# Sums of weight blocks made in place, raw w2 tiles, and bias and early preparation in the m1 steps of a two-layer-pair kernel

## The chip, the cores and the metric

One core of one Trainium2 chip runs the whole program. The metric is the device time of one execution in microseconds, as the median of several runs.

## The reference

Two kinds of layer alternate, each twice, with a residual sum around each. S = 2048 tokens, D = 1024, F = 3584, all float32.

```python
def A(q, k, v, shift_k, ssm_k, ssm_D):       # q is the layer norm of x
    kv = short_causal_conv(k, shift_k) * v   # 4 taps per channel
    y = long_causal_conv(kv, ssm_k)          # 2048 taps per channel, by FFT in the reference
    return q * (y + kv * ssm_D)

def B(x, w1, b1, w2, b2):                    # x is the layer norm of x
    h = einsum("bsd,df->bsf", x, w1) + b1
    h = where(h > 0, h, 0) ** 2
    return einsum("bsf,fd->bsd", h, w2) + b2

x = x + A(ln(x)); x = x + B(ln(x)); x = x + A(ln(x)); x = x + B(ln(x))
```

The result of the long convolution is the same in both A layers, so the kernel computes it once.

## The kernel before

**Blocks.** Tokens go in four blocks of 512, and each layer pair A, B handles a block at a time. `ORDER` lists the eight blocks (layer pair, token block): block 0 is (0, 0), and blocks 5, 6, 7 are (0, 3), (1, 2), (1, 3). The long convolution runs beside blocks 0 to 4; its products are made on GpSimd (POOL) and its other work on all engines. It is finished early in the second half of block 4.

**Steps.** A block is a list of steps, each with one weight tile of 128 x 512. An m1 step multiplies a w1 tile with the normalized input `xh`, `xl` (12 matmuls). Numbers are split into a high and a low fp32r part, and three matmuls make one product (`mm3`). After two m1 steps (kh = 0, 1) one F tile of 128 rows is complete, and `relu2` or `relu_w` makes its squared ReLU, `rh`, `rl`.

**Blocks 5 to 7 (`WINO`)** use a 2 x 2 block product with seven products in place of eight, as Strassen and Winograd did. Their F tiles go in pairs, `WCH = (3, 3, 4, 4)` pairs to a chunk. In each chunk the m1 steps come first (12, 12, 16, 16), and then seven groups j of w2 steps, one step per pair (21, 21, 28, 28 steps, 6 matmuls each), which accumulate in two PSUM banks. `evict_w` adds these to `acc` (or `fx`, `fg`) after each group. Three of the seven groups use w2 tiles as they are; four use sums of w2 blocks ("t" tiles, tensors `td`).

**Weights.** A weight goes one of two ways. Raw: SyncE (SP) loads 256 KB into `wr` (eight buffers) up to `W_LOAD` = 8 steps ahead, ScalarE (ACT) casts it to the high part of `whl` (six buffers), and VectorE (DVE) subtracts to make the low part; this pair of operations is the split. Pair: a split that was stored in DRAM (`wd_m1_...`, `wd_m2_...`, `wd_t_...`) is loaded whole, 512 KB, `W_PAIR` = 4 steps ahead. `from_pair` decides; about half of the weights are kept as pairs. A pair's load waits until PE has ended the step that used its buffer.

**What sets the order.** There is no scheduler in these blocks: the loop over steps writes all instructions, and each engine and SP's DMA queue runs its own in that order. `lag.at(k, f)` calls f k ticks later; a tick is a step, with a few more at the first w2 step of a chunk, which waits for `relu_w`. So SP, which issues every load and store, is one queue in order: a DMA that waits for an engine holds back all that stand behind it.

**Other work in these blocks.**
- `load_b2`, `add_b2w`: loads b2 (broadcast over partitions) into a `px` buffer, and POOL adds it to the residual in `acc` and `fk` (eight additions of 128 x 512).
- `prep_a`: from step 29 of a block on, loads the next block's four input token tiles into `px` (two buffers) and makes their statistics (`stats`), three steps apart.
- `prep_w`: the rest of the next block's preparation. `early` loads x and the convolution's result y (`YD`), combines them (`combine`, four operations), makes new statistics and stores x to `X1`. `late` loads `X1`, normalizes, transposes on PE and splits into the next `xh`, `xl`.
- `make_t`: makes the "t" tiles in 28 parts, each with two loads of w2 (256 KB), four differences of 128 x 256 on DVE and two stores (256 KB) to `TD`. It is a generator, advanced once per step from the convolution's end on.

In the weight buffers' names, wd_m1_1_2_1 is the pair of w1, F tile 7 x 1 + 2, half kh = 1.

Of the kernel before, what the change touches and what calls it, by code (L numbers as in the profile page):

```python
# [233 lines left out]
def tile_h3_mlp(ctx: ExitStack, tc: tile.TileContext, q, kT, vT, shk, ssmT, ssmD, w1, b1, w2, b2,  # L234
# [556 lines left out]

    def load_xy(l, b, tt):
        x, y = load_x(l, b, tt), []
        for h in range(2):
            yt = ml.tile([P, 512], F32, name="yt", bufs=2)
            SY.dma_start(yt, YD[b][:, tt, h * 512:(h + 1) * 512])
            y.append(yt)
        return x, y

    def combine(x, y, m, r):  # L800
        for h in range(2):
            sl = slice(h * 512, (h + 1) * 512)
            V.scalar_tensor_tensor(y[h], x[:, sl], m, y[h], op0=OP.subtract, op1=OP.mult)
            V.scalar_tensor_tensor(x[:, sl], y[h], r, x[:, sl], op0=OP.mult, op1=OP.add)
# [594 lines left out]
    def make_t():  # L1399
        parts = [(p, dq) for p in range(FT // 2) for dq in range(2)]  # L1400
        got = {}

        def load(n):
            if n < len(parts):
                p, dq = parts[n]
                got[n] = []
                for e in range(2):
                    pool, nm, m = (const, ("fh", "fl")[e], 1) if n % 2 else (cv, "sm", 2)
                    t = pool.tile([P, 2, 256], F32, name=nm, bufs=m)
# [7 lines left out]
        yield
        yield
        yield
        for n, (p, dq) in enumerate(parts):  # L1420
# [9 lines left out]
            yield  # L1430
            SY.dma_start(TD[p][:, 0:2, dq * 256:(dq + 1) * 256], t[0])
            yield
            SY.dma_start(TD[p][:, 2:4, dq * 256:(dq + 1) * 256], t[1])
            load(n + 2)
# [420 lines left out]
```

## Time and profile before

| | us |
|---|---|
| median of three runs | 2807.38 |
| the three runs | 2803.62, 2807.38, 2811.40 |
| the profiled execution | 2809.33 |
| its span, first to last instruction | 2807.6 |
| TensorE busy in the span | 2706.5 |
| granted TensorE clock, mean | 0.987 |

DMA moved 782.04 MB, 279 GB/s over the span. Block 4 begins at about 1560 us of the span, block 5 at 1877.8, block 6 at 2202.4, block 7 at 2508. In the views PE is TensorE, DVE VectorE, ACT ScalarE, POOL GpSimd; SPq is SP's DMA queue. A line of the windows view gives the stretch, its length, busy time (and count) of PE, PEld, DVE, ACT and POOL, then the granted clock, the share of time that the DMA engines were busy, and GB/s. A line of the waits view gives who waited for whom, the sum in us, how often, and the longest. A line of the timeline gives start, duration, engine, line, operation, and in brackets the idle time before it with what ended it.

### The profile page before, as it was taken

How to read it: one execution, taken by the hardware profiler on the slowest of the kernel's cores; microseconds unless marked ns; L12 is line 12 of the kernel's file. 1: busy time of each engine (PE TensorE's matmuls, PEld its weight loads, DVE VectorE, ACT ScalarE, POOL GpSimd, SP SyncE). 2: the span in 40 equal slices, each digit the busy share in tenths (PEclk: the TensorE clock that was granted, in tenths of full speed). 3: DMA queues.
4: the chain of work that ended last, by engine and by line, in shares of the span. 5: the costliest groups of instructions: out<-in, count | busy, mean ns of one | idle time of the engine just before them, and what ended most of it. 6: DMA issues, size and time to landing. Idle time of an engine off the chain costs nothing.

```text
span 2807.6 us, 36324 instructions
## 1 busy us (share of the span) xinstructions
PE 2706.5 (96%) x12532; PEld 2237.1 (80%) x12532; DVE 1942.1 (69%) x3009; ACT 1067.6 (38%) x1835; POOL 926.4 (33%) x655
## 2 busy tenths in 40 slices
PE   7799899799999999999999999999999999999999
PEld 6688787688888788888888888887777778777887
DVE  8868789777777877779767754366576655664545
ACT  4254344333334233442234322243335433343433
POOL 6826665155542555336552553001000000001000
PEclk9999999999999999999999999999999999999999
DMA  8589999789988898888977786778988876776565
GB/s 259 167 288 356 363 330 322 259 269 353 298 280 304 281 338 283 274 320 289 353 247 274 292 308 218 237 265 312 339 271 293 290 243 235 239 251 228 202 214 199
DMA packets 380025, 782.04 MB, mean 279 GB/s; under 512 B 43832, under 2 KB 160704, under 8 KB 379840
## 3 DMA queue, kind: packets, MB, share of 16 engines
q1 hardware_dynamic: 379840, 779.71, 81.2%
q8 instruction: 99, 1.62, 0.2%
q14 instruction: 86, 0.70, 0.1%
HBM read 629.62 MB, written 149.95 MB: 278 GB/s over the span
## 4 chain that ended last, share of the span: by engine, by line
PE 76%; DMA 9%; DVE 9%; issue 2%; POOL 2%; SPq 1%; ACT 1%; DVEq 0%; ACTq 0%; POOLq 0%
PE p L323 23%; PE p L322 23%; PE p L324 23%; DMA whl<-wd_m 2%; DVE whl L999 2%; DMA wd_m<-whl 1%; DMA wr<-w 1%; PE pt L323 1%; PE pt L324 1%; PE pt L322 1%; DMA wr<-td 1%; DMA cg<-gd 1%; DMA td<-yt 1%; DMA whl<-wd_t 1%; DMA acc<-x 1%
## 5 line engine op out<-in xcount | busy, mean ns | idle before, releaser
L512 POOL TENSOR_TENSOR cp<-cx,cg 128x384 f32<-128x384 f32 (+5 forms) x288 | 540.1, 1888 | 585.6 <-DVE sm L516 361.1
L322 PE MATMUL p<-xh,whl 128*128 128x512 f32 (+1 forms) x1840 | 708.7, 385 | 3.6 <-DMA whl<-wd_m 2.0
L324 PE MATMUL p<-xh,whl 128*128 128x512 f32 (+1 forms) x1840 | 704.8, 383 | 1.7 <-DVE whl L999 1.1
L323 PE MATMUL p<-xl,whl 128*128 128x512 f32 (+1 forms) x1840 | 704.5, 383 | 0.3 <-DVE xl L1312 0.3
L323 PE MATMUL p<-whl,rh 128*128 128x512 f32 x1372 | 546.3, 398 | 15.5 <-DVE whl L999 15.3
L322 PE MATMUL p<-whl,rh 128*128 128x512 f32 x1372 | 549.6, 401 | 9.0 <-DMA whl<-wd_m 6.9
L324 PE MATMUL p<-whl,rl 128*128 128x512 f32 x1372 | 544.2, 397 | 0.0
L991 ACT CAST whl<-wr 128x512 fp32r<-128x512 f32 x538 | 325.9, 619 | 502.2 <-PE p L324 251.3
L999 DVE TENSOR_TENSOR whl<-wr,whl 128x512 fp32r<-128x512 f32 x524 | 431.9, 840 | 86.3 <-ACT whl L991 80.9
L322 PEld LDWEIGHTS p<-xh,whl 128*128 128x128 f32 x1840 | 347.3, 189 | 72.8 <-DMA whl<-wd_m 3.6
L324 PEld LDWEIGHTS p<-xh,whl 128*128 128x128 f32 x1840 | 347.1, 189 | 70.3 <-DVE whl L999 1.6
L323 PEld LDWEIGHTS p<-xl,whl 128*128 128x128 f32 x1840 | 347.2, 189 | 66.0 <-DVE xl L1312 0.5
L323 PEld LDWEIGHTS p<-whl,rh 128*128 128x128 f32 x1372 | 260.5, 190 | 80.3 <-DVE whl L999 23.0
L322 PEld LDWEIGHTS p<-whl,rh 128*128 128x128 f32 x1372 | 260.5, 190 | 70.2 <-DMA whl<-wd_m 6.4
L324 PEld LDWEIGHTS p<-whl,rl 128*128 128x128 f32 x1372 | 260.3, 190 | 60.4
L1396 DVE TENSOR_TENSOR rl<-wr,rh 128x512 fp32r<-128x512 f32 x140 | 146.0, 1043 | 216.6 <-ACT rh L1391 216.5
L1490 POOL TENSOR_TENSOR acc<-acc,px 128x512 f32<-128x512 f32 x18 | 29.6, 1677 | 777.5 <-DMA wr<-td 602.0
L516 DVE TENSOR_REDUCE sm<-cp 128x128 f32<-128x384 f32 (+5 forms) x288 | 249.5, 874 | 21.6 <-POOL cp L512 21.6
L1388 ACT ACTIVATE wr<-p,b1t 128x512 f32<-128x512 f32 x138 | 95.2, 690 | 373.7 <-PE p L324 372.6
L1454 DVE TENSOR_TENSOR rl<-wr,rh 128x256 fp32r<-128x256 f32 x84 | 46.9, 558 | 228.6 <-ACT rh L1449 228.3
L1513 DVE TENSOR_TENSOR acc<-p,acc 128x512 f32<-128x512 f32 x152 | 101.0, 687 | 81.7 <-PE p L324 81.1
L1446 ACT ACTIVATE wr<-p,b1t 128x512 f32<-128x512 f32 x84 | 57.9, 690 | 198.4 <-PE p L324 198.2
(250 smaller groups left out, 3427.7 us busy)
## 6 DMA issues: line engine op xcount, KB each, us to landing
whl<-wd_m SPq DMA_DIRECT2D x482, 512.0 KB, 5.2
wr<-w SPq DMA_DIRECT2D x394, 256.0 KB, 5.5
wr<-td SPq DMA_DIRECT2D x152, 256.0 KB, 4.3
wd_m<-whl SPq DMA_DIRECT2D x70, 512.0 KB, 6.2
cx<-xd SPq DMA_DIRECT2D x48, 512.0 KB, 5.1
cg<-gd SPq DMA_DIRECT2D x48, 512.0 KB, 7.4
gd<-fg SPq DMA_DIRECT2D x72, 256.0 KB, 6.3
cx<-xd SPq DMA_DIRECT2D x48, 384.0 KB, 5.8
```

Source lines behind the costliest of these rows:

```text
L322: PE.matmul(o, lh, rh, start=start, stop=False)
L323: PE.matmul(o, lh, rl, start=False, stop=False)
L324: PE.matmul(o, ll, rh, start=False, stop=stop)
L512: G.tensor_mul(pr.rearrange("p c i -> p i c"), xt[:, 0:j + 1], gt[:, j::-1])
L516: V.tensor_reduce(sm[:, ty, jj], st["pr"], axis=AX.X, op=OP.add)
L991: A.copy(t[:, 0], raws[n]["t"])
L999: ENG[e[n % len(e)]].tensor_sub(t[:, 1], raws[n]["t"], t[:, 0].bitcast(F32))
L1388: A.activation(r, st["o"], AF.Relu, bias=b1t[:, st["f"]:st["f"] + 1])
L1396: V.tensor_sub(st["lo"], st["r"]["t"], st["hi"].bitcast(F32))
L1446: A.activation(r, st["o"], AF.Relu, bias=b1t[:, st["f"]:st["f"] + 1])
L1454: V.tensor_sub(st["lo"], r[:, 0:n], st["hi"].bitcast(F32))
L1513: V.tensor_add(accs[tt][:, d], o, accs[tt][:, d])
```

## The change

- `make_t` forms its differences in the tiles that it loaded. The first ten parts lie in the buffers that the convolution has left (`cp`, `cx`, `cg`), the others in `sm`, `fh`/`fl` and `yt` in turn. The order in `TD` changes, and `T_AT` maps it. It is advanced once per m1 step and 0.6 times per w2 step, and also in block 4's last 18 steps (0.6).
- All w2 weights of chunks 0 to 2 in blocks 5 to 7, 24 pairs a block among them, are loaded raw (`single`).
- b2 is loaded and added 22 ticks later: in the m1 steps of chunk 1, where it was in chunk 0's w2 steps.
- `early` runs in the m1 steps of chunks 2 and 3, where it was spread over 13 steps each, and loads y into a `px` buffer. `late` moves by a step or two.

```diff
-W_PREP, W_XN = 84, 32
-T_KEPT = 10
+W_PREP, W_EARLY, W_LATE = 90, (87, 80, 45, 38), 30
+T_KEPT, T_RATE, T_FIRST, T_AT = 10, 0.6, 10, (0, 3, 1, 2)
...
         def early(tt, k):
             st = sts[tt]
             if k == 0:
-                st["x"], st["y"] = load_xy(l, b, tt)
-                ytbusy[0] = True
+                st["x"] = load_x(l, b, tt)
+                st["y"] = pre.tile([P, D], F32, name="px", bufs=2)
+                SY.dma_start(st["y"], YD[b][:, tt])
...
         for tt in range(NT):
             for k, d in enumerate((0, 4, 5, 7)):
-                lag.at(13 * tt + d + 1, early, tt, k)
+                lag.at(W_PREP - W_EARLY[tt] + d, early, tt, k)
             for k, d in enumerate((0, 5, 7, 8, 9)):
-                lag.at(W_PREP - W_XN + 6 * tt + d, late, tt, k)
+                lag.at(W_PREP - W_LATE + 5 * tt + d, late, tt, k)
...
+                    if c < len(WCH) - 1:
+                        single.add(len(wsrc) - 1)
...
     def from_pair(w):
-        return split_kept(wsrc[w]) and w - first_w[wsrc[w]] >= PAIR_GAP
+        return w not in single and split_kept(wsrc[w]) and w - first_w[wsrc[w]] >= PAIR_GAP
...
+        def places(n):
+            if n < T_FIRST:
+                nm, m = (("cp", 3), ("cx", 2), ("cg", 2))[n % 3]
+                t = cv.tile([P, 2, 2, 256], F32, name=nm, bufs=m)
+                return [t[:, 0], t[:, 1]]
+            return [pool.tile([P, 2, 256], F32, name=nm, bufs=m) for pool, nm, m in (
+                [(cv, "sm", 2)] * 2, [(const, "fh", 1), (const, "fl", 1)], [(ml, "yt", 2)] * 2)[n % 3]]
...
-            t = [ml.tile([P, 2, 256], F32, name="yt", bufs=2) for _ in range(2)]
-            V.tensor_sub(t[0][:, 0], b[0][:, 1], b[0][:, 0])
-            V.tensor_sub(t[0][:, 1], b[1][:, 1], t[0][:, 0])
+            (b00, b01), (b10, b11) = (tuple(t[:, h] for h in range(2)) for t in got[n])
+            V.tensor_sub(b00, b01, b00)
+            V.tensor_sub(b01, b11, b01)
             yield
-            V.tensor_sub(t[1][:, 0], b[1][:, 1], b[0][:, 1])
-            V.tensor_sub(t[1][:, 1], b[1][:, 0], t[0][:, 1])
+            V.tensor_sub(b11, b11, b00)
+            V.tensor_sub(b10, b10, b11)
             yield
...
-                lag.at(12, load_b2, bst)
-                lag.at(16, add_b2w, bst, wacc)
+                lag.at(34, load_b2, bst)
+                lag.at(38, add_b2w, bst, wacc)
...
-        if tgen and (left > 18 or u in WINO):
-            next(tgen[0], None)
+        if tgen:
+            town += T_RATE if k == "w2" or u not in WINO and left <= 18 else 1
+            while town >= 1:
+                town -= 1
+                next(tgen[0], None)
```

Two places show how the order moves.

SP's queue in block 6, where chunk 0's w2 steps end and chunk 1's m1 steps begin (px<-x are the x tiles for the next block's statistics, wd_m_1_2_1 is the pair of chunk 1's eighth m1 step; brackets name the engines and DMAs that the row waits for). Before:

```order
L989 DMA whl<-wd_m_0_6_0_1735 128x1024 [waits DMAHW3_49,DVE_49,PE_49]
L710 DMA px<-x_112 128x1024 [waits DMAHW4_49]
L710 DMA px<-x_112 128x1024 [waits DMAHW5_49,Pool_49]
L989 DMA whl<-wd_m_1_0_0_2009 128x1024 [waits DMAHW6_49,DVE_49,PE_49]
L989 DMA whl<-wd_m_1_0_1_2046 128x1024 [waits DMAHW7_49,PE_49]
L710 DMA px<-x_112 128x1024 [waits DMAHW4_49,DMAHW0_49,DVE_49]
L989 DMA whl<-wd_m_1_1_0_2315 128x1024 [waits DMAHW1_49,PE_49]
L989 DMA whl<-wd_m_1_1_1_2346 128x1024 [waits DMAHW2_49,PE_49]
L989 DMA whl<-wd_m_1_2_0_2376 128x1024 [waits DMAHW3_49,PE_49]
L710 DMA px<-x_112 128x1024 [waits DMAHW5_49,DVE_49]
L989 DMA whl<-wd_m_1_2_1_2425 128x1024 [waits PE_49,Activation_49]
```

And with the change:

```order
L983 DMA whl<-wd_m_0_6_0_1735 128x1024 [waits DMAHW6_49,DVE_49,PE_49]
L710 DMA px<-x_112 128x1024 [waits DMAHW7_49]
L710 DMA px<-x_112 128x1024 [waits DMAHW0_49]
L983 DMA whl<-wd_m_1_0_0_2009 128x1024 [waits DMAHW1_49,DVE_49,PE_49]
L1617 DMA px<-b 128x1024 [waits DMAHW7_49,DMAHW2_49,DVE_49]
L983 DMA whl<-wd_m_1_0_1_2046 128x1024 [waits DMAHW3_49,PE_49,Activation_49]
L710 DMA px<-x_112 128x1024 [waits DMAHW4_49,DMAHW0_49,DVE_49]
L983 DMA whl<-wd_m_1_1_0_2315 128x1024 [waits DMAHW5_49,PE_49,Activation_49]
L983 DMA whl<-wd_m_1_1_1_2346 128x1024 [waits DMAHW6_49,PE_49,Activation_49]
L983 DMA whl<-wd_m_1_2_0_2376 128x1024 [waits PE_49]
L710 DMA px<-x_112 128x1024 [waits DMAHW2_49,Pool_49]
L983 DMA whl<-wd_m_1_2_1_2425 128x1024 [waits DMAHW1_49,PE_49,Activation_49]
```

The b2 load (px<-b) now stands among the x loads. It takes the buffer of the first x tile, so it waits for that tile's statistics on DVE; the fourth x load takes the buffer of b2, so it waits for POOL, for the last of the eight additions. Before, the wait for POOL stood at the second x load, some 13 steps after the additions.

DVE's order in block 5, where the early preparation of a token tile (the operations on px) stands. Before, in chunk 2's w2 steps, with evictions (acc), splits (whl) and make_t's differences (yt<-fh) around it:

```order
L1497 TENSOR_TENSOR acc<-p_18922,acc 128x512
L1497 TENSOR_TENSOR acc<-p_18923,acc 128x512
L999 TENSOR_TENSOR whl<-wr,whl 128x512
L803 SCALAR_TENSOR_TENSOR yt<-px,mv,yt 128x512
L804 SCALAR_TENSOR_TENSOR px<-yt,rs,px 128x512
L803 SCALAR_TENSOR_TENSOR yt<-px,mv,yt 128x512
L804 SCALAR_TENSOR_TENSOR px<-yt,rs,px 128x512
L999 TENSOR_TENSOR whl<-wr,whl 128x512
L1425 TENSOR_TENSOR yt<-fh 128x256
```

And with the change, in chunk 2's m1 steps, between the parts of `relu_w` (rl):

```order
L1424 TENSOR_TENSOR fl<-fl,fh 128x256
L1425 TENSOR_TENSOR fl<-fl 128x256
L1451 TENSOR_TENSOR rl<-wr,rh 128x256
L795 SCALAR_TENSOR_TENSOR px<-px,mv 128x512
L796 SCALAR_TENSOR_TENSOR px<-px,rs 128x512
L795 SCALAR_TENSOR_TENSOR px<-px,mv 128x512
L796 SCALAR_TENSOR_TENSOR px<-px,rs 128x512
L993 TENSOR_TENSOR whl<-wr,whl 128x512
L681 BN_STATS st<-px 128x6 x2
L682 BN_AGGR mv_18642<-st 128x2
L687 TENSOR_SCALAR ve<-mv_18642 128x1
L1451 TENSOR_TENSOR rl<-wr,rh 128x512
```

The same four operations now stand between m1 steps' work, with no eviction near them, and make_t's differences write the tiles that they read.

More of the change, by code (lines that the diff above doesn't have):

```diff
@@ L790, in prep_b @@
         return xh, xl
[L792 to L798, printed above, removed]
     def combine(x, y, m, r):
@@ L802, in combine @@
             sl = slice(h * 512, (h + 1) * 512)
-            V.scalar_tensor_tensor(y[h], x[:, sl], m, y[h], op0=OP.subtract, op1=OP.mult)
-            V.scalar_tensor_tensor(x[:, sl], y[h], r, x[:, sl], op0=OP.mult, op1=OP.add)
+            V.scalar_tensor_tensor(y[:, sl], x[:, sl], m, y[:, sl], op0=OP.subtract, op1=OP.mult)
+            V.scalar_tensor_tensor(x[:, sl], y[:, sl], r, x[:, sl], op0=OP.mult, op1=OP.add)
     def prep_w(l, b, lag):
@@ L813, in early @@
             if k == 0:
-                st["x"], st["y"] = load_xy(l, b, tt)
-                ytbusy[0] = True
+                st["x"] = load_x(l, b, tt)
+                st["y"] = pre.tile([P, D], F32, name="px", bufs=2)
+                SY.dma_start(st["y"], YD[b][:, tt])
             elif k == 1:
                 combine(st["x"], st.pop("y"), mv[:, tt, 0:1], r[:, tt:tt + 1])
-                ytbusy[0] = False
             elif k == 2:
@@ L867, in tile_h3_mlp @@
     HALF = ((0, 1), (2, 3))
-    steps, wsrc = [], []
+    steps, wsrc, single = [], [], set()
     def add(kind, u, c, a, i, tts=ALL, w=None):
@@ L947, in from_pair @@
     def from_pair(w):
-        return split_kept(wsrc[w]) and w - first_w[wsrc[w]] >= PAIR_GAP
+        return w not in single and split_kept(wsrc[w]) and w - first_w[wsrc[w]] >= PAIR_GAP
     ring, now = [], [0]
-    tgen, made, ytbusy = [], set(), [False]
+    tgen, made = [], set()
     def room():
@@ L977, in w_load @@
                 next(tgen[0])
-            SY.dma_start(raw, TD[c][:, a])
+            SY.dma_start(raw, TD[c][:, T_AT[a]])
         elif k == "m1":
@@ L1405, in load @@
                 p, dq = parts[n]
[L1406 to L1409, printed above, removed]
+                got[n] = places(n)
+                for e, t in enumerate(got[n]):
                     f = 2 * p + e
@@ L1412, in load @@
                     SY.dma_start(t, src[:, :, dq * 256:(dq + 1) * 256])
-                    got[n].append(t)
         load(0)
+        yield
         load(1)
@@ L1418, in make_t @@
         yield
-        yield
         for n, (p, dq) in enumerate(parts):
-            b = got.pop(n)
-            while ytbusy[0]:
-                yield
-            t = [ml.tile([P, 2, 256], F32, name="yt", bufs=2) for _ in range(2)]
-            V.tensor_sub(t[0][:, 0], b[0][:, 1], b[0][:, 0])
-            V.tensor_sub(t[0][:, 1], b[1][:, 1], t[0][:, 0])
-            yield
-            V.tensor_sub(t[1][:, 0], b[1][:, 1], b[0][:, 1])
-            V.tensor_sub(t[1][:, 1], b[1][:, 0], t[0][:, 1])
[L1430 to L1434, printed above, removed]
+            (b00, b01), (b10, b11) = (tuple(t[:, h] for h in range(2)) for t in got[n])
+            V.tensor_sub(b00, b01, b00)
+            V.tensor_sub(b01, b11, b01)
+            yield
+            V.tensor_sub(b11, b11, b00)
+            V.tensor_sub(b10, b10, b11)
+            yield
+            load(n + 2)
+            yield
+            if n >= T_FIRST:
+                yield
+            for e, t in enumerate(got.pop(n)):
+                SY.dma_start(TD[p][:, 2 * e:2 * e + 2, dq * 256:(dq + 1) * 256], t)
             if dq:
                 made.add(p)
-            yield
             yield
@@ L1647, in tile_h3_mlp @@
             lo_u = hi_u
-    owed = 0.0
+    owed = town = 0.0
     fowed = 0.0
```

## Prediction

> **What bounds the kernel now.** I read the shares by engine first, then the windows cut at the blocks, then who TensorE (PE) waited for in each window, and last the timelines around the long waits.
>
> ```profile
> PE 2706.5 (96%) x12532; PEld 2237.1 (80%) x12532; DVE 1942.1 (69%) x3009; ACT 1067.6 (38%) x1835; POOL 926.4 (33%) x655
> core 0: us, PE busy (x) PEld busy (x) DVE busy (x) ACT busy (x) POOL busy (x), PEclk, DMA share, GB/s
> 1572.00:1877.80 305.80, 305.80 (x1374) 251.73 (x1373) 167.88 (x245) 96.37 (x165) 97.39 (x57) 1.00 0.76 261
> 1877.80:2112.60 234.80, 216.15 (x901) 172.09 (x899) 151.89 (x302) 86.45 (x141) 11.76 (x8) 0.97 0.89 311
> ...
> 2202.40:2420.00 217.60, 211.86 (x907) 170.95 (x908) 126.32 (x223) 86.34 (x142) 13.43 (x8) 0.99 0.73 249
> ...
> 2508.00:2720.00 212.00, 209.30 (x903) 168.83 (x904) 103.04 (x162) 85.36 (x137) 13.92 (x8) 1.00 0.66 219
> ```
>
> PE bounds the span, so only its idle time and a lowered clock can be won. The change acts on block 4 (first window, nearly all of it; PE never idle) and on blocks 5, 6 and 7. The other windows are their chunks 0 to 2, where all w2 weights become raw. Idle there: 234.80 - 216.15 = 18.65, 217.60 - 211.86 = 5.74, 212.00 - 209.30 = 2.70 us. The clock takes (1 - 0.97) x 234.8 = 7.0 and 0.01 x 217.6 = 2.2 us more. That is 36.3 us, the most that the change can win. The waits of PE, for these three windows in turn:
>
> ```profile
> PE p L322 <- DMA whl<-wd_m: 9.2, 5, 3.2
> PE p L323 <- DVE whl L999: 8.9, 8, 1.7
> PE p L322 <- DVE acc L1497: 0.5, 1, 0.5
> ...
> PE p L323 <- DVE whl L999: 5.7, 5, 2.2
> PE p L322 <- DMA whl<-wd_m: 0.6, 1, 0.6
> ...
> PE p L323 <- DVE whl L999: 2.4, 2, 2.2
> PE p L322 <- DVE whl L999: 1.4, 1, 1.4
> ```
>
> Two causes: pairs that land late (block 5, where DMA is busy 0.89) and splits on VectorE (DVE) that come late. Why they are late:
>
> ```profile
> 2239.05 10.04 POOL L1490 TENSOR_TENSOR acc<-acc,px 128x512 f32<-128x512 f32 x6 [309.73 <-DMA wr<-td]
> 2240.59 3.47 DVE L999 TENSOR_TENSOR whl<-wr,whl 128x512 fp32r<-128x512 f32 x2
> 2251.25 1.28 DVE L1497 TENSOR_TENSOR acc<-p,acc 128x512 f32<-128x512 f32 x2
> 2252.45 1.88 DVE L999 TENSOR_TENSOR whl<-wr,whl 128x512 fp32r<-128x512 f32 x3
> ...
> 2248.01 0.79 PE L323 MATMUL p<-whl,rh 128*128 128x512 f32 x1 [2.23 <-DVE whl L999]
> 2249.03 0.63 PE L322 MATMUL p<-whl,rh 128*128 128x512 f32 x1
> 2249.46 0.63 PE L323 MATMUL p<-whl,rh 128*128 128x512 f32 x1
> ...
> 2071.60 0.74 DVE L803 SCALAR_TENSOR_TENSOR yt<-px,mv,yt 128x512 f32<-128x512 f32 x1
> 2073.89 0.75 DVE L804 SCALAR_TENSOR_TENSOR px<-yt,rs,px 128x512 f32<-128x512 f32 x1
> 2074.56 0.69 DVE L999 TENSOR_TENSOR whl<-wr,whl 128x512 fp32r<-128x512 f32 x1
> 2075.30 0.51 PE L323 MATMUL p<-whl,rh 128*128 128x512 f32 x1 [1.22 <-DVE whl L999]
> ```
>
> In block 6 a split takes 1.74 us while GpSimd (POOL) adds the bias, and 0.63 us when it has ended: the engines slow each other. PE waits 2.23 us, and then starts matmuls 0.43 us apart instead of 0.23, for some ten of them: 2 us more. In block 5 the early preparation's four operations (2071.60 to 2074.6) stand ahead of a split, and PE waits 1.22 us.
>
> **The change part by part.** The bias leaves the w2 steps of chunk 0 for the m1 steps of chunk 1, and early preparation goes into m1 steps of chunks 2 and 3. An m1 step asks little of DVE: in chunk 1 eleven of twelve weights come as finished pairs. The m1 stage of chunk 1 in block 6:
>
> ```profile
> 2270.00:2304.00 34.00, 34.00 (x152) 28.10 (x151) 15.52 (x35) 12.13 (x20) 0.00 (x0) 1.00 0.84 293
> ```
>
> DVE is busy 15.52 of 34 us. In 13 us of bias adds 13/34 of that, 5.9 us, becomes 2.8 times (1.74/0.63) as long, 16.6 us: 3.6 us late, caught up in the stage's remaining 20 us, before w2 steps read what relu_w makes. I cost the move at nothing on DVE. Its bound above is those 3.6 us in each of three blocks, if the adds end late in the stage.
>
> Early preparation now takes x and y both from the two px buffers, so a y load waits on SP until the X1 store of the token tile before it has landed:
>
> ```profile
> x<-px SPq DMA_DIRECT2D x24, 512.0 KB, 5.3
> ```
>
> 5.3 us are two m1 steps. Behind it stand a raw tile for the eighth step from there and a pair for the fifth: hidden, 0. Without that lead it would be 5.3 us four times.
>
> The Trainium skill (SBUF — State Buffer, Who interferes with whom) says that a Vector instruction with two SBUF inputs contends with a GpSimd instruction that reads SBUF, and one with a single SBUF input does not. The rows agree: the split slows, the eviction from PSUM at 2251.25 keeps its 0.64 us each. The rule speaks against the change, since relu_w's differences have two SBUF inputs and contend in m1 steps as well. By the rule the adds would run there at the rate between that of block 7 and the faster one of block 5 shown below, which moves the sum by 1 to 2 us through the gate described next.
>
> Raw tiles: 72 pairs fewer (24 a block, 512 KB each), 72 raw tiles of 256 KB more, 72 casts and 72 splits more. At 0.63 us the splits are 45 us of DVE. The cover is in chunk 1 of block 6, where 12 of 21 steps are already raw:
>
> ```profile
> 2304.00:2333.00 29.00, 29.00 (x126) 23.25 (x125) 19.33 (x32) 9.19 (x15) 0.00 (x0) 1.00 0.65 208
> ```
>
> PE is busy for all of it, DVE for 19.33 of 29 us. Nine more splits make 25.0, nine casts (0.62 each) bring ScalarE (ACT) to 14.8: hidden, cost 0, at the latest until DVE is full. In block 5 make_t adds about 2.5 parts of four 0.42 us differences, 4.2 us, in such a chunk: 29.2 of 29, just full. I take 1 us exposed in each of its three chunks, 3 us; bounds 0 and the 9 x 3 added splits, 17 us.
>
> make_t itself keeps its loads, differences and stores. It starts no part in yt before part 10, runs on through block 4's last 18 steps (DVE 167.88 of 305.80 us there: hidden), and has 13 parts loaded ahead of block 5 where it had 9. Four parts of 1.05 MB, and 24 x 256 KB of pairs, take 10.5 MB out of block 5's window (311 GB/s over 234.8 us are 73 MB); its 9.2 us of late pairs I count as gone, since the raw loads are asked for eight steps ahead where pairs were four. Two waits at hand-overs (0.6 and 1.4 us) stay. So 36.3 - 3 - 2.0 = 31 us are won, if nothing new waits.
>
> **The new wait (the gate).** In blocks 5 and 6 the order puts b2 into the two px buffers between the x tiles of the next block's statistics: the b2 load waits for the first statistics, and the fourth x load waits for the last of the eight bias adds. SyncE (SP) issues in order. Behind that x load stands the pair of the eighth m1 step of chunk 1 (wd_m1_1_2_1), and everything later.
>
> ```profile
> 2263.90 0.90 SPq L710 DMA_DIRECT2D px<-x  x2
> 2270.34 0.39 PE L322 MATMUL p<-xh,whl 128*128 128x512 f32 x1
> 2270.83 1.29 DVE L681 BATCH_NORM_STATS2 st<-px 128x6 f32<-128x512 f32 x2 [2.66 <-DMA px<-x]
> ...
> 1877.77 0.39 PE L322 MATMUL p<-xh,whl 128*128 128x512 f32 x1
> 1880.51 0.39 PE L322 MATMUL p<-xh,whl 128*128 128x512 f32 x1
> ...
> px<-b SPq DMA_DIRECT2D x8, 512.0 KB, 7.0
> whl<-wd_m SPq DMA_DIRECT2D x482, 512.0 KB, 5.2
> ...
> DMA to landing us min/median/max: 3.1/5.3/10.6
> ...
> 1917.55 9.12 POOL L1490 TENSOR_TENSOR acc<-acc,px 128x512 f32<-128x512 f32 x6 [175.53 <-DMA px<-b]
> 1926.63 2.68 POOL L1490 TENSOR_TENSOR fk<-fk,px 128x512 f32<-128x512 f32 x2
> 2544.75 10.42 POOL L1490 TENSOR_TENSOR acc<-acc,px 128x512 f32<-128x512 f32 x6 [292.28 <-DMA wr<-td]
> 2555.14 3.53 POOL L1490 TENSOR_TENSOR fk<-fk,px 128x512 f32<-128x512 f32 x2
> ...
> 1948.00:1982.00 34.00, 32.54 (x143) 26.38 (x142) 19.37 (x45) 11.38 (x18) 0.00 (x0) 1.00 1.01 373
> ```
>
> Count from the first m1 matmul of chunk 1 (2270.34 in block 6). An m1 step is 1880.51 - 1877.77 = 2.74 us, so the eighth begins at 7 x 2.74 = 19.2. The statistics end at 2270.83 + 1.29, so 1.8. b2 lands 7.0 later: 8.8. The adds take 11.8 us (block 5) to 13.95 (block 7): to 20.6 or 22.8. The pair lands 5.2 later: 25.8 or 28.0. PE would wait 6.6 to 8.8 us. Against that, x has about two pairs fewer ahead of it (1 MB, 2.8 us at the 373 GB/s of the last row), and the pair may land on an idle queue in the 3.1 us that are the least of all loads of that line. With both in full and the quick adds the wait is 6.6 - 2.8 - 2.1 = 1.7 us. I take 5.5, nearer to the upper end, since the x load is one of two that share their way, and 2 us for the clock after it: 7.5 in block 6. In block 5 DMA is full in this stage (share 1.01): the easings fail, the wait is 8 us, and what SP could not issue meanwhile lands late as well, so with the clock I take 11 us. Block 7 prepares no next block and has no such x load. Together 18.5 us; bounds 0 (all hidden, with b2 asked for a little earlier still) and 2 x (8.8 + 2 + 3) = 28, where 3 us are 1 MB of backlog.
>
> Sum: 31 - 18.5 = 12.5 us less than the profiled execution's 2809.33 us (span 2807.6): 2796.8. That execution is 1.95 us above the median of the three runs, 2807.38, so I forecast 2794 us.
>
> **Rivals.** (1) The gate is hidden: adds at the fastest rate of block 5 and x and b2 on light queues. Then 31 us are won: 2776. For it: DMA loses 18.9 MB. Against: b2 is asked for only behind the statistics, and 7.0 us of landing and 11.8 of adds already fill the 19.2. (2) Slower: the added splits make DVE the bound of w2 steps, since each of seven evictions stands ahead of splits that PE needs three steps later. All 72 exposed at 0.69 us are 50 us: 2794 + 50 = 2844. It decides against the change when more than 30 of them are exposed (12.5 + 8.4 = 21 us). Against: the 29 us window with 12 raw steps and no wait. (3) No change to measure (within 0.3%, which is 8.4 us, about the least that can be told here): the gate costs its upper bound, 28 us, and the splits half of theirs, 8: 36.3 - 2.0 - 8 - 28 = -1.7, so 2809. For it: both the gate and the full DVE stand in block 5, which holds 25.7 of the 36.3 us. Against: the upper bounds would have to come together.
>
> **How the numbers follow.** The gate between 10 and 25 us with most of the idle time won (2787 to 2801): 0.55. Hidden (2774 to 2787): 0.2. Rival 3 (2801 to 2816): 0.17. Slower: 0.08. Two in ten left out give 2775 to 2808. Faster than 2799: all of the hidden case and most of the first, 0.68; same 0.24; slower 0.08.
>
> **What would show it.** Right: PE's waits for DVE whl in blocks 5 to 7 fall below 5 us; the split keeps 0.63 us in w2 steps; and PE waits 4 to 9 us for DMA whl<-wd_m once each in blocks 5 and 6, about 19 us into chunk 1's m1 steps, with SP silent for over 10 us ahead of it. Wrong: no such wait (rival 1), or many waits of under 2 us on DVE whl in the all-raw chunks (rival 2).

## The result and the profile after

| | before | after |
|---|---|---|
| median, us | 2809.39 (4 runs, 2803.62 to 2812.24) | 2774.14 (4 runs, 2770.91 to 2780.61) |
| profiled execution, us | 2809.33 (span 2807.6) | 2772.34 (span 2770.6) |
| granted clock, mean | 0.987 | 0.990 |

The ratio is 0.988, with a 95% interval of 0.9854 to 0.9905. On a second chip the same two kernels gave 2811.04 and 2773.94 us, ratio 0.9869 (0.9851 to 0.9886). So the change wins about 36 us. The forecast was 2794 us, and 2774 lies just below its range.

The shares by engine and the windows view of the kernel after, cut like before at blocks 4 and 5 to 7 (chunks 0 to 2 of the latter); columns as explained with the profile before:

```profile
PE 2693.8 (97%) x12532; PEld 2234.8 (81%) x12532; DVE 1960.4 (71%) x3081; ACT 1106.8 (40%) x1907; POOL 919.2 (33%) x655
```

```profile
1572.00:1882.20 310.20, 310.20 (x1393) 255.36 (x1392) 176.80 (x264) 97.92 (x168) 99.70 (x58) 1.00 0.80 275
1882.20:2091.20 209.00, 207.74 (x902) 168.75 (x901) 152.32 (x300) 99.35 (x164) 10.26 (x8) 1.00 0.87 299
2181.00:2388.50 207.50, 207.19 (x900) 169.05 (x901) 127.26 (x231) 99.04 (x164) 10.22 (x8) 1.00 0.66 223
2476.20:2683.10 206.90, 206.88 (x901) 169.11 (x902) 110.46 (x187) 98.63 (x161) 10.21 (x8) 1.00 0.60 198
```

The same work of PE (901 or so matmul rows a window) takes 209.0, 207.5 and 206.9 us, where it took 234.8, 217.6 and 212. PE idles 1.3, 0.3 and 0.0 us, and the clock is 1.00 in all three. DVE does 72 operations more (3081 against 3009), and POOL's additions are shorter: 10.2 us a block against 11.76 to 13.92. What PE waited for in blocks 5 to 7 (1878 to 2775 us of the span, here and in the experiments; the last 30 us or so of a longer run's block 7 are left out), before and then after:

```profile
PE p L323 <- DVE whl L999: 17.0, 15, 2.2
PE p L322 <- DMA whl<-wd_m: 12.3, 9, 3.2
```

```profile
PE p L322 <- DMA whl<-wd_m: 4.5, 8, 1.4
PE p L322 <- ACT wr L1443: 0.9, 1, 0.9
PE p L323 <- DVE whl L993: 0.3, 1, 0.3
```

The waits for splits are gone but for 0.3 us, and of the waits for pairs some third is left. A stage is a run of m1 or of w2 steps; its length is taken from its first matmul to that of the next stage in PE's timeline, in us:

| | m1 c0 | w2 c0 | m1 c1 | w2 c1 | m1 c2 | w2 c2 | m1 c3 | w2 c3 | block |
|---|---|---|---|---|---|---|---|---|---|
| 5 before | 32.66 | 39.15 | 33.27 | 36.01 | 43.68 | 50.11 | 43.66 | 46.09 | 324.63 |
| 5 after | 32.66 | 29.35 | **34.69** | 29.46 | 43.55 | 39.22 | 44.00 | 45.97 | 298.90 |
| 6 before | 32.77 | 35.17 | 32.67 | 29.46 | 43.55 | 42.26 | 43.68 | 45.93 | 305.49 |
| 6 after | 32.76 | 29.36 | **33.19** | 29.44 | 43.55 | 39.14 | 43.54 | 44.16 | 295.14 |
| 7 before | 32.77 | 33.88 | 32.67 | 29.46 | 43.55 | 39.13 | 43.64 | 40.68 | 295.78 |
| 7 after | 32.74 | 29.36 | 32.66 | 29.45 | 43.53 | 39.14 | 43.54 | 40.04 | 290.46 |

Block 7's stages after are undisturbed (m1 of chunk 0 within 0.1 us), and I measure all others by 32.67, 29.35, 32.67, 29.45, 43.54 and 39.14 us, 206.9 us for chunks 0 to 2. The gate of the prediction (SP held by an x load that waits for POOL's additions, and the pairs behind it late) is there, in bold, but it is small. Its rows in block 6, from the timelines of SP's queue, POOL and PE:

```profile
2236.76 0.90 SPq L710 DMA_DIRECT2D px<-x  x2
...
2242.61 0.33 SPq L1617 DMA_DIRECT2D px<-b  x1
...
2257.30 0.32 SPq L710 DMA_DIRECT2D px<-x  x1
2257.72 1.73 SPq L983 DMA_DIRECT2D whl<-wd_m  x2
...
2247.05 7.71 POOL L1487 TENSOR_TENSOR acc<-acc,px 128x512 f32<-128x512 f32 x6 [288.81 <-DMA px<-b]
2254.73 2.54 POOL L1487 TENSOR_TENSOR fk<-fk,px 128x512 f32<-128x512 f32 x2
...
2243.20 0.39 PE L322 MATMUL p<-xh,whl 128*128 128x512 f32 x1
...
2262.65 0.50 PE L322 MATMUL p<-xh,whl 128*128 128x512 f32 x1 [0.23 <-DMA whl<-wd_m]
```

SP stands still from 2247.1 to 2257.3, as long as POOL adds, and the pair of the eighth m1 step is asked for right behind. That step is due at 2243.20 + 19.2 = 2262.4 us, and PE waited 0.23 us for it. The chain is as forecast; each link is shorter. In block 5 the pair of the eighth step came just in time. The 2.0 us lost there hold a wait of 0.40 us for the ninth step's pair and one of 0.85 us for ScalarE (ACT), 6 us later; whether the second comes from the gate too, the profile doesn't show.

### The profile page after: what moved, and what is told of

Its sections match the earlier page's. It is cut to its first block, busy times and chain, and to the rows that moved or that the text cites. A ratio compares the mean times of both kernels' runs of the same rounds, so it can differ in the third digit from the quotient of the medians.

```text
span 2770.6 us, 36545 instructions
## 1 busy us (share of the span) xinstructions
PE 2693.8 (97%) x12532; PEld 2234.8 (81%) x12532; DVE 1960.4 (71%) x3081; ACT 1106.8 (40%) x1907; POOL 919.2 (33%) x655
## 4 chain that ended last, share of the span: by engine, by line
PE 78%; DMA 7%; DVE 7%; POOL 3%; issue 2%; SPq 2%; ACT 1%; DVEq 0%; POOLq 0%; ACTq 0%
PE p L322 24%; PE p L323 24%; PE p L324 24%; DMA whl<-wd_m 2%; DMA cg<-gd 1%; DMA cx<-xd 1%; PE pt L323 1%; DVE whl L993 1%; PE pt L324 1%; PE pt L322 1%; DMA wd_m<-whl 1%; DMA gd<-fg 1%; DVE sm L516 1%; DMA wr<-w 1%; POOL cp L512 1%
## 5 line engine op out<-in xcount | busy, mean ns | idle before, releaser
L323 PE MATMUL p<-xl,whl 128*128 128x512 f32 (+1 forms) x1840 | 704.6, 383 | 0.3 <-DVE xl L1306 0.3
L985 ACT CAST whl<-wr 128x512 fp32r<-128x512 f32 x610 | 367.8, 619 | 467.3 <-PE p L324 243.9
L323 PE MATMUL p<-whl,rh 128*128 128x512 f32 x1372 | 543.7, 396 | 3.6 <-DVE whl L993 3.6
L993 DVE TENSOR_TENSOR whl<-wr,whl 128x512 fp32r<-128x512 f32 x596 | 458.8, 790 | 74.2 <-ACT whl L985 70.4
L323 PEld LDWEIGHTS p<-xl,whl 128*128 128x128 f32 x1840 | 347.0, 189 | 66.2 <-DVE xl L1306 0.5
L323 PEld LDWEIGHTS p<-whl,rh 128*128 128x128 f32 x1372 | 260.0, 190 | 63.0 <-DVE whl L993 5.1
L1487 POOL TENSOR_TENSOR acc<-acc,px 128x512 f32<-128x512 f32 x18 | 23.2, 1321 | 772.9 <-DMA px<-b 772.9
L1451 DVE TENSOR_TENSOR rl<-wr,rh 128x256 fp32r<-128x256 f32 x84 | 48.6, 579 | 209.1 <-ACT rh L1446 209.0
```

The source lines that it names most:

```text
L323: PE.matmul(o, lh, rl, start=False, stop=False)
L985: A.copy(t[:, 0], raws[n]["t"])
L993: ENG[e[n % len(e)]].tensor_sub(t[:, 1], raws[n]["t"], t[:, 0].bitcast(F32))
L1451: V.tensor_sub(st["lo"], r[:, 0:n], st["hi"].bitcast(F32))
```

## Experiments

**The changed kernel once more.** No edit.

> The changed kernel once more, nothing edited, beside the three below. Theory (the gate is on its edge): m1 of chunk 1 in blocks 5 and 6, ideally 32.67 us, again takes somewhere between 33 and 42 us, not the 34.69 and 33.19 of the first profile; all other stages within 0.3 us of it except the last w2 stage of a block (43 to 47 us); time 2771 to 2786 us. Rival (the gate has a fixed price, and the four edits above differed through the edits): 34.7 and 33.2 again within 0.5 us.

Measured: 2773.94 us (4 runs, 2771.53 to 2774.89), and m1 of chunk 1 at 35.41 and 37.61 us, where the first profile had 34.69 and 33.19. No other stage of chunks 0 to 2 differs by over 0.1 us. PE's timeline in block 6, and its waits in this stage of block 5:

```profile
2263.47 0.50 PE L322 MATMUL p<-xh,whl 128*128 128x512 f32 x1 [3.03 <-DMA whl<-wd_m]
```

```profile
PE p L322 <- DMA whl<-wd_m: 1.1, 2, 0.8
PE p L322 <- ACT wr L1443: 0.8, 1, 0.8
```

So with unchanged code the gate (stage length over 32.67 in blocks 5 and 6 together) was 2.5 us in one execution and 7.7 in another, on another chip: it stands on its edge. In block 6 b2 landed 0.4 us later than in the first profile (4.83 against 4.44), the additions took 0.5 us longer (10.72 against 10.25), and the pair came 1.9 us later (6.8 us after its issue against 4.9); that makes the 2.8 us between waits of 3.03 and 0.23. That the wait costs 4.9 us where it lasts 3.03 is mostly the clock: the granted clock was 0.59 over the 4.1 us behind it, and matmuls ran slower.

**Each bias addition done twice** (so the bias goes in twice in blocks 5 to 7).

```diff
-                G.tensor_add(a, a, st["t"][:, h * 512:(h + 1) * 512])
+                for _ in range(2):
+                    G.tensor_add(a, a, st["t"][:, h * 512:(h + 1) * 512])
```

> The changed kernel with each of the eight bias additions of a block done twice on POOL, so the bias goes in twice in blocks 5 to 7. It lengthens POOL's row from 10.25 us to 20.5 us and nothing else. Theory (the fourth x load waits for POOL's additions, and the pair behind it on SP for that load): the whole 10.25 us shows on PE in m1 of chunk 1 of block 5 and of block 6, plus 2 us of lowered clock in each where the wait was short until now, and nothing in block 7: m1 there 44 to 47 us and 43 to 46 us against 34.7 and 33.2, block 7 stays at 32.67; time +20 to +25 us against the changed kernel. Rival (the additions are hidden, and what PE waits for is the landing of the pair alone): less than 5 us.

Measured: 2800.50 us (2797.12 to 2802.80), +26.6 against the changed kernel beside it; a little more than the range, since the stage goes up to 47.73 and 47.28 us and stays 32.67 in block 7. (The sixteen additions take 22.8 us, where 20.5 were expected.) The timelines of POOL, SP and PE in block 5:

```profile
1951.78 16.61 POOL L1488 TENSOR_TENSOR acc<-acc,px 128x512 f32<-128x512 f32 x12 [202.18 <-DMA px<-b]
1968.34 6.28 POOL L1488 TENSOR_TENSOR fk<-fk,px 128x512 f32<-128x512 f32 x4
...
1974.64 0.32 SPq L710 DMA_DIRECT2D px<-x  x1
1975.06 0.37 SPq L983 DMA_DIRECT2D whl<-wd_m  x1
...
1979.60 0.80 PE L322 MATMUL p<-xh,whl 128*128 128x512 f32 x1 [13.02 <-DMA whl<-wd_m]
```

The x load leaves 0.02 us after the last addition (1968.34 + 6.28 = 1974.62), the pair 0.42 us after it, and PE starts 4.5 us later. Added time on POOL, an engine that is 33% busy in the changed kernel, comes out on PE nearly in full, in the two blocks that have the x load and not in the third. The mechanism of the gate is shown by this.

**x first.** The statistics of the next block begin 20 places earlier, so all four x loads stand ahead of b2.

```diff
-            if n == 28:
+            if n == (8 if u in WINO else 28):
                 pa = prep_a(*ORDER[u + 1])
-            elif n > 28 and pa is not None and next(pa, 0) == 0:
+            elif n > 8 and pa is not None and next(pa, 0) == 0:
```

> The changed kernel with the statistics of the next block's x begun 20 places earlier in blocks 5 and 6 (place 8 of the block in place of 28), so that all four x loads stand ahead of the bias load in SP's queue. All the arithmetic stays. Theory (gate): m1 of chunk 1 falls to 32.67 us in both blocks, in every profile; w2 of chunk 0, where the statistics now run on DVE, stays within 1 us of 29.35; time 2 to 6 us below the changed kernel run beside it, and a narrower spread. Rival (DVE is so full in w2 of chunk 0 that the four statistics push out its splits): m1 of chunk 1 at 32.67 us too, but w2 of chunk 0 3 to 6 us longer; time as the changed kernel or above.

Measured: 2770.82 us (2768.46 to 2772.82), ratio 0.986 (0.9845 to 0.9876): 3.1 us below the changed kernel run beside it, though the intervals of the two ratios overlap, so that the gain in time isn't shown for certain. The stage is 32.66 and 32.67 us: the gate is gone. Part of that went to w2 of chunk 0 in block 5, 30.90 us against 29.35, where the statistics stand before splits. PE's waits in blocks 5 to 7:

```profile
PE p L322 <- DMA whl<-wd_m: 3.1, 5, 1.2
PE p L323 <- DVE whl L993: 0.8, 3, 0.3
```

The waits for pairs that are left stand in chunk 3's w2 steps, 2.4 us in block 5 and 0.6 in block 6.

**x earlier still in block 5.**

```diff
-            if n == (8 if u in WINO else 28):
+            if n == ({5: 2, 6: 8}.get(u, 28)):
```

> The kernel with x first (e7_x_first) with one number changed: in block 5 the statistics begin at place 2 of the block in place of 8, so that three of the four fall in chunk 0's m1 steps, where DVE has room. Theory: w2 of chunk 0 in block 5, 30.9 us with x first, falls to 29.4, m1 of chunk 1 stays at 32.67 us in both blocks; time 1 to 2 us below x first, about 2769 us, the least of all kernels here. Rival (the x loads at that place meet the four output stores and delay raw tiles): m1 or w2 of chunk 0 2 to 4 us longer than 32.66 and 29.35.

Measured: 2774.47 us (2767.49 to 2776.78), ratio 0.9869 (0.9851 to 0.9886). The theory missed: w2 of chunk 0 became 34.15 us, not 29.4. The timelines of SP and PE there:

```profile
1908.47 0.33 SPq L710 DMA_DIRECT2D px<-x  x1
...
1914.94 2.34 SPq L972 DMA_DIRECT2D wr<-td  x3
...
1921.36 0.50 PE L322 MATMUL p<-whl,rh 128*128 128x512 f32 x1 [2.47 <-ACT whl L985]
```

And SP's first raw tile of a w2 sum with x first:

```profile
1910.63 0.33 SPq L972 DMA_DIRECT2D wr<-td  x1
```

It is the gate again in another place. The fourth x load waits until the statistics of the second tile end, and SP, silent since 1900.6, issues the raw tiles for the first w2 steps 34.5 us into the block (begun at 1880.47), where x first has 26.8 (1910.63 less 1883.83). PE waits 2.47 us for the cast of such a tile, and a lowered clock behind it brings the stage to 4.8 us over.

**The bias back in chunk 0** (the change without its move).

```diff
-                lag.at(34, load_b2, bst)
-                lag.at(38, add_b2w, bst, wacc)
+                lag.at(12, load_b2, bst)
+                lag.at(16, add_b2w, bst, wacc)
```

> The changed kernel with one part undone: b2 is loaded and added at ticks 12 and 16 again, in chunk 0's w2 steps. Theory (the change wins by taking three loads off VectorE and DMA in the w2 steps; the additions of POOL are one of them): the splits of chunk 0 slow to about 1.7 us while POOL adds, and chunk 0's w2 stage grows from 29.4 us by 5 to 8 us in each of blocks 5, 6 and 7; the gate of the fourth x load goes, which is worth about 2 us in block 5 and 0.5 in block 6. Sum about +15 us: 2789 us. Rival (DMA alone was the cause, since 19 MB fewer are moved): no longer w2 stage, 2772 to 2776 us.

Measured: 2784.75 us (2782.62 to 2787.31), ratio 0.9905 (0.9891 to 0.9920). w2 of chunk 0 is 35.75, 35.88 and 35.18 us, 18.8 us over the undisturbed stages, and m1 of chunk 1 is 32.67: gate gone, waits for DVE back:

```profile
PE p L323 <- DVE whl L993: 11.7, 4, 4.8
```

**The bias moved alone** (the kernel before, with only that edit).

> The kernel before with only the bias moved from chunk 0's w2 steps to chunk 1's m1 steps (ticks 34 and 38). Theory: w2 of chunk 0 falls from 39.15, 35.17 and 33.88 us to 31-33, 29.4 and 29.4 us, about 17 us in all; the gate appears in m1 of chunk 1 of blocks 5 and 6 (5 to 10 and 3 to 7 us, DMA being as busy as before: more pairs, more of make_t's traffic); net -1 to -9 us. Rival (the predicted price of the gate, 11 + 7.5 us, holds for the loaded queues of the kernel before): net 0 to +3. Rival (the bias was hidden in chunk 0 and splits were late for another reason): w2 of chunk 0 keeps over 33 us and the time goes up by the gate, +5 to +15.

Measured: 2801.02 us (7 runs, 2795.26 to 2808.17) beside 2810.93, ratio 0.9966 (0.9953 to 0.9979): -9.9 us, just past the theory's end. w2 of chunk 0 is 32.17, 29.58 and 29.35 us. The gate is 4.2 and 2.6 us, less than the theory had, on queues as full as before. POOL in block 5:

```profile
1952.36 7.86 POOL L1490 TENSOR_TENSOR acc<-acc,px 128x512 f32<-128x512 f32 x6 [207.98 <-DMA whl<-wd_m]
1960.18 2.90 POOL L1490 TENSOR_TENSOR fk<-fk,px 128x512 f32<-128x512 f32 x2
```

Eight additions take 10.7 us in place of the 11.8 that they took in chunk 0 of the same block, and 10.9 and 10.2 in blocks 6 and 7 in place of 13.5 and 13.9, with all else as before: it is the move that makes them quicker.

**Pairs back** (the change without raw w2 tiles).

```diff
-                    if c < len(WCH) - 1:
+                    if c < 0:
                         single.add(len(wsrc) - 1)
```

> The changed kernel with one part undone: the 72 w2 weights are loaded as stored pairs again where before they were. Theory: pairs matter where DMA is full, in block 5, which loses 5 to 12 us; blocks 6 and 7 stay within 2 us: 2779 to 2786 us. Rival (VectorE bounds the w2 steps, so 72 splits fewer help): blocks 6 and 7 get shorter and the time falls below 2770 us.

Measured: 2777.26 us (2776.24 to 2783.31), ratio 0.9883 (0.9868 to 0.9898). The w2 stages of chunks 0 to 2 are longer only in block 5 (30.12, 30.10, 40.71 us, 2.9 in all); the gate was 4.5 and 4.6 us. The loss in block 5 is less than the 5 to 12 us of the theory, and the interval holds those of the changed kernel: what the raw tiles are worth beside the other edits isn't clear of the noise.

**Raw tiles alone** (the kernel before, with only `single`).

> The kernel before with raw tiles alone (all w2 weights of chunks 0 to 2 raw, 24 pairs a block fewer; bias, early preparation and make_t as before). Theory (the 72 added splits need the room on DVE that the other edits make): w2 of chunk 1, where nothing else runs, falls to 29.5 us in block 5 (from 36.0), but w2 of chunk 0 and chunk 2, where the bias and the early preparation still stand, stays within 3 us of its 39.2, 35.2, 33.9 and 50.1, 42.3, 39.1 us, up or down; net -3 to -10 us. Rival (raw tiles do it all, since late pairs were the cause): w2 of chunks 0 and 2 fall as well, by 5 us or more in block 5; net -15 us or more. Rival (DVE becomes the bound): they rise by 3 us each; net +5 to +15.

Measured: 2802.36 us (8 runs, 2800.87 to 2806.89), ratio 0.9976 (0.9966 to 0.9985), -8.6 us. w2 of chunk 1 in block 5 falls to 30.91; chunk 0 keeps 37.27, 32.53 and 32.43, chunk 2 48.79, 42.13 and 39.14. What remains is DVE:

```profile
PE p L323 <- DVE whl L1001: 21.2, 14, 4.9
PE p L322 <- DMA whl<-wd_m: 3.4, 6, 0.9
```

The waits for pairs fall from 12.3 to 3.4 us, and those for splits rise from 17.0 to 21.2: part of the gain turns into the other wait, until the bias and the early preparation leave these steps.

**Early preparation spread again**, 13 steps a token tile.

```diff
-W_PREP, W_EARLY, W_LATE = 90, (87, 80, 45, 38), 30
+W_PREP, W_EARLY, W_LATE = 90, (83, 70, 57, 44), 30
```

> The changed kernel with the early preparation at its former places (one token tile every 13 steps from 7 steps after the start of the preparation's count, so that parts of it fall into chunk 2's and 1's w2 steps); y stays in a px buffer. Theory: its four combining operations stand ahead of splits again, and chunk 2's w2 stage grows by 5 to 9 us in block 5 and by about 3 us in block 6; block 7 prepares nothing and stays: 2782 to 2786 us. Rival (the place does not matter once the additions of POOL are gone): within 2 us of 2774.

Measured: 2782.19 us (2779.52 to 2786.00), ratio 0.9897 (0.9882 to 0.9912). w2 of chunk 2 is 46.47 and 42.10 us in blocks 5 and 6, 7.3 and 3.0 over the undisturbed; the gate was 1.9 and 4.9 us.

**make_t at full rate.**

```diff
-T_KEPT, T_RATE, T_FIRST, T_AT = 10, 0.6, 10, (0, 3, 1, 2)
+T_KEPT, T_RATE, T_FIRST, T_AT = 10, 1.0, 10, (0, 3, 1, 2)
```

> The changed kernel with make_t advanced once per step in w2 steps too, as before (0.6 in the change). Theory: VectorE is just full in block 5's w2 stages, and two thirds more of make_t in them cost 2 to 5 us in block 5 alone, until make_t has run out: 2776 to 2779 us. Rival: VectorE has room, 2774 us and block 5's stages unchanged.

Measured: 2781.98 us (2779.98 to 2785.57), ratio 0.9893 (0.9876 to 0.9909). w2 of chunk 1 in block 5 is 31.43 us, 2 more; m1 of chunk 1 there is 41.81, 9.1 more: with make_t's loads and stores between the pairs the gate, which the theory here had left out, comes near the 11 us that I had forecast for this block in the changed kernel. PE's waits for pairs in blocks 5 to 7:

```profile
PE p L322 <- DMA whl<-wd_m: 11.3, 8, 5.2
```

**All w2 weights raw, chunk 3 too.**

```diff
-                    if c < len(WCH) - 1:
+                    if True:
                         single.add(len(wsrc) - 1)
```

> The changed kernel with the block products of chunk 3 on raw tiles too, so that no pair of w2 is read back anywhere in blocks 5 to 7. All the arithmetic stays. Theory (what is left at a block's end is PE waiting for pairs whose loads come late): w2 of chunk 3, 45.97, 44.16 and 40.04 us in the first profile against 39.13 where nothing waits, falls by 2 to 5 us in blocks 5 and 6; time 4 to 8 us below. Rival (DVE has no room there beside the next block's preparation): DVE-whl waits appear in chunk 3's w2 and it gets longer, as it was in chunk 0 and 2 of the kernel before; time 5 to 15 us above.

Measured: 2776.10 us (2774.16 to 2778.89), not 4 to 8 below 2773.94, and not 5 above. w2 of chunk 3 is 45.62, 45.79 and 42.15 us (before this edit 44.89, 43.62 and 40.62 on the same chip). In blocks 5 and 6 one wait of 2.17 us for a split stands near the stage's end, where the pairs were late before:

```profile
2177.32 0.50 PE L323 MATMUL p<-whl,rh 128*128 128x512 f32 x1 [2.17 <-DVE whl L993]
...
2473.34 0.50 PE L323 MATMUL p<-whl,rh 128*128 128x512 f32 x1 [2.17 <-DVE whl L993]
```

Late pairs are exchanged for late splits. What I took for waits in that stage, 45.97 and 44.16 us against 39.14 where nothing else runs, is mostly not idle time. The groups of PE's operations in the last w2 stage of block 6, kernel after:

```profile
L322 PE MATMUL p<-whl,rh 128*128 128x512 f32 x24 | 9.7, 403 | 0.7 <-DMA whl<-wd_m 0.7
...
L838 PE MATMUL p<-ident,px 128*128 128x128 f32 x32 | 4.1, 272 | 0.0
```

The 32 transposes of `late` take 4.1 us, and block 7, which prepares no next block, has none: some 4 of the 5 to 7 us are work.

**The kernel before once more.** No edit.

> The kernel before, nothing edited, for a second profile of it: block 5 began at 1877.77 us in its first profile and at 1878.6 to 1882.2 us in those of the changed kernel and its variants with the whole of it. If blocks 0 to 4 pay for what now runs in block 4's last 18 steps, block 5 begins again at 1877 to 1878.5; if it is the spread of blocks 0 to 4, anywhere from 1877 to 1883. Its stages of blocks 5 to 7 again within 2 us of 324.6, 305.5 and 295.8 us.

Measured: 2810.30 us, ratio to the others 1.0001 (0.9991 to 1.0011). Block 5 begins at 1880.12 us. The changed kernel's two profiles have 1882.18 and 1880.17, so the 4.4 us between the first two profiles were spread, and no cost shows of what now runs in block 4's end. One of 2 or 3 us would not: over all fourteen profiles block 5 begins anywhere from 1877.8 to 1885.4. Its blocks are 320.38, 303.97 and 297.14 us; block 5 is 4.2 us under the first profile's, more than the 2 us that I expected. PE's waits in them:

```profile
PE p L323 <- DVE whl L999: 18.2, 15, 2.3
PE p L322 <- DMA whl<-wd_m: 9.3, 9, 2.3
```

## Why the prediction was wrong, point by point

The sum of the prediction against two pairs of profiles: the first of before and after, and the second of both. All in us; over the undisturbed 206.9 us a block for chunks 0 to 2.

| term | forecast | first pair | second pair |
|---|---|---|---|
| idle and clock in chunks 0 to 2 of before | -36.3 | -41.6 | -37.7 |
| waits at hand-overs that stay | +2.0 | 0 | 0 |
| added splits exposed | +3 | 0 | 0 |
| gate | +18.5 | +2.5 | +7.7 |
| chunk 3 | 0 | -2.4 | -2.5 |
| blocks 0 to 4 | 0 | +4.4 | 0 |
| sum | -12.8 | -37.1 | -32.5 |

**The step that failed is the size of the gate.** The mechanism was right, in its place and its order: SP silent for 10 us, the pair of the eighth m1 step behind the x load, PE waiting there in block 6, and nothing of it in block 7. The prediction said 7.5 us in block 6 and 11 in block 5; the two profiles have 0.5 and 4.9, and 2.0 and 2.7. The other terms made 8.3 us more of the 24.3 us that the first pair's sum was out (36.3 us too low, 5 us of costs that didn't come, and chunk 3, less the 4.4 us by which blocks 0 to 4 were longer). By its own links in block 6, first profile:

- "The statistics end ... 1.8" after the first m1 matmul of chunk 1. They ended at 2242.6, 0.6 before it: 2.4 us sooner. The x load took 4.5 us from issue to statistics (2236.76 to 2241.29), not the 6.9 of the row before.
- "b2 lands 7.0 later". It landed 4.4 later (2242.61 to 2247.05, where POOL starts): 2.6 sooner. The 7.0 was the median over all eight blocks' b2 loads. In the kernel before, SP issued b2 of block 6 behind five loads of the residual, 2.5 MB, and POOL began 9.3 us later (2239.05); at the new place two x loads and two pairs were issued in the 6.2 us ahead of it. That the queue made the difference is argued from this:

```profile
2225.32 1.82 SPq L1480 DMA_DIRECT2D acc<-x  x3
2227.19 1.06 SPq L1485 DMA_DIRECT2D fk<-x  x2
...
2229.72 0.65 SPq L1620 DMA_DIRECT2D px<-b  x1
```

- "The adds take 11.8 us (block 5) to 13.95 (block 7)". They took 10.25: 1.55 to 3.7 less. Additions were dear where DVE worked beside them. DVE was busy for all 13.47 us of block 6's additions before, and for 1.36 of 10.22 us now:

```profile
2239.05:2252.52 13.47, 9.92 (x35) 7.05 (x34) 13.47 (x11) 6.03 (x11) 13.43 (x8) 0.87 0.42 131
...
2247.05:2257.27 10.22, 10.22 (x46) 8.45 (x45) 1.36 (x2) 3.68 (x6) 10.21 (x8) 1.00 0.56 221
...
2250.68 0.44 DVE L1451 TENSOR_TENSOR rl<-wr,rh 128x256 fp32r<-128x256 f32 x1 [5.16 <-ACT rh L1446]
2256.34 1.48 DVE L1451 TENSOR_TENSOR rl<-wr,rh 128x512 fp32r<-128x512 f32 x1 [5.22 <-ACT rh L1446]
```

  The last two rows are all that DVE did in these 10 us. Both have two SBUF inputs. The second took 1.48 us beside the additions, where its line takes 0.69 without them; the first kept the 0.42 to 0.44 us of its shape. So one of the two agrees with the rule of the Trainium skill (SBUF — State Buffer, Who interferes with whom). I had weighed it with the DVE load averaged over the whole stage (15.52 of 34 us) rather than in the 10 us at hand, and from it I had refused the additions a rate better than any seen.
- "The pair lands 5.2 later": 4.9 us (2257.72 to 2262.6).

Together 6.9 us less, so that the 6.6 us of wait, the lower end of the forecast's count, become nearly nothing (0.23 measured). The forecast had then allowed for easings of 2.8 and 2.1 us and credited 1.1. The 2 us for the clock didn't come either in the first profile, where the granted clock stayed at 1.00. In block 5 b2 landed in 4.5 us, the additions took 10.3 and the pair some 4.6; DMA was busy for 0.92 of that stage, where the forecast had 1.01, and the backlog came to a wait of 0.40 us for the ninth step's pair. The bias and its additions had been priced by rows of the crowded place that they were leaving, and the landings of b2 and the pair by medians over whole kernels. Rival 1 named the condition that came true ("adds at the fastest rate of block 5 and x and b2 on light queues") and gave 2776 us, but I gave it 0.2, on the ground that 7.0 + 11.8 filled the 19.2 us. That argument used the same two rows again. That its time comes so near is in part chance: the gate still cost 2.5 us, and 41.6 us, not 31, were to be won.

**36.3 us, "the most that the change can win"**, was too low by 5.3 us for that profile. In block 7 idle time and a clock of 1.00 gave 2.70 us, and the stages give 4.6. It isn't the clock, which was granted in full there (1.00 over 2552.40:2555.80 too, behind the wait of 2.23 us). A matmul's row in the profile lasts 0.39 us while the next one starts 0.23 us after it, so idle time counts only from 0.16 us into a wait, and the row behind a wait takes 0.1 us more. Rows of such a step in block 7, kernel before:

```profile
2553.66 0.39 PE L322 MATMUL p<-whl,rh 128*128 128x512 f32 x1
2554.09 0.50 PE L323 MATMUL p<-whl,rh 128*128 128x512 f32 x1
2554.43 0.39 PE L324 MATMUL p<-whl,rl 128*128 128x512 f32 x1
```

L323 is the first matmul of a step that needs the split's low part. It starts 0.43 us after the one before it, and the next one 0.34 us later: 0.3 us a step, in several steps on end, none of it idle time by the profile. The length of the same stage where nothing disturbs it (29.36 against 33.88) holds all of it.

**The added splits cost nothing**, not 3 us. The one wait for a split that is left in blocks 5 to 7 is 0.31 us, and w2 of chunk 1 in block 5, which I had put at 29.2 of 29 us of DVE, takes 29.46 us. With make_t at full rate the same stage gets 2 us longer, with a wait of 0.62 us for a split, so the margin is small. The bound of 17 us and rival 2 are far off.

**Right:** the bias slowed the splits (undone, 18.8 us return in the w2 stages, and the time rises by 7 to 11); of make_t's earlier parts and y in `px` no more shows in the m1 stages of chunks 2 and 3 than the 0.5 us (0.8 in the second profile) by which m1 of chunk 3 in block 5 is longer; block 4 shows no gain and no loss clear of its spread; late pairs are gone from chunks 0 to 2 but for the gate.

**Not seen:** chunk 3 became 2.4 us shorter. Why, no run shows. No part carries the whole: undone one at a time they give back 7 to 11 (bias), 5 to 8 (early preparation), 4 to 8 (make_t's rate) and 1 to 3 us (raw tiles), and alone the raw tiles won 8.6 and the bias 9.9. In each of the four pairs the first figure goes by the ratios to the kernel before on the same chip and the second by the medians, which come from two chips; the last pair lies within the noise.

## What to carry to other kernels

When work is moved, price it where it arrives: a landing time or a contended rate from the old place holds the old place's queue and neighbours, and a median over eight loads hides which of them queue. For a chain of such links, look at each link's least row beside its median before calling the sum full, and if slack and chain differ by a few microseconds expect executions to differ by as much. And in a queue that issues in order, put a load that waits for another engine behind everything that PE needs soon; here a move of four loads ahead of the additions ended the gate, and a further move built another.

To know what waits cost, compare a stage with its undisturbed twin in the same trace; idle time plus the lowered clock is less than the loss.

## What the runs showed of the hardware

Whether a wait of 2 to 3 us lowers TensorE's clock isn't settled by its length. With all w2 weights raw, two waits of 2.17 us stood at the same place of blocks 5 and 6. Behind the first the granted clock stayed at 1.00, and over the 4 us from the restart after the second it was 0.57:

```profile
2177.30:2181.00 3.70, 3.68 (x16) 3.01 (x17) 3.15 (x5) 0.62 (x1) 0.00 (x0) 1.00 0.92 331
...
2473.30:2477.30 4.00, 3.96 (x10) 3.15 (x11) 3.02 (x5) 0.62 (x1) 0.00 (x0) 0.57 0.84 318
```

In the kernel before, the wait of 2.23 us in block 6 that the prediction shows lowered it (0.59 over 2247.20:2250.60), and one as long in block 7 did not. With raw tiles alone, waits of 2.91 and 2.80 us did not, and there the stages lost 3.2 and 3.1 us, 0.3 more than the waits. What else decides, no run shows.

Where the clock is lowered, its price doesn't grow with the wait. After 13.02 us of idle PE, matmuls came 0.43 us apart for eight of them, and at 0.23 again 3.6 us after the restart at 1979.60:

```profile
1980.20 0.63 PE L323 MATMUL p<-xl,whl 128*128 128x512 f32 x1
1980.62 0.63 PE L324 MATMUL p<-xh,whl 128*128 128x512 f32 x1
...
1983.18 0.40 PE L324 MATMUL p<-xh,whl 128*128 128x512 f32 x1
1983.42 0.39 PE L322 MATMUL p<-xh,whl 128*128 128x512 f32 x1
```

The stage lost 15.06 us, 2.0 more than the wait. After 3.03 us of idle it lost 4.94, 1.9 more. The Trainium skill (TensorE: Matmul & The Clock Gate, Part 1: The HAM clock gate) puts the clock at half after an idle window of some 3.4 us, and back after as long a busy one; the way back agrees (3.6 us), while here idle times of 2.17, 2.23 and 3.03 us were enough to lower it, and others of 2.17 to 2.91 us were not.
